# A fused attention, routed experts and gated layer on one core: casts of the last stage's weights on ScalarE, no router places in two blocks, list positions compared in bf16 pairs

## The chip, the cores and the metric

One core of one Trainium2 chip runs the whole program as a single launch. Its engines are TensorE (PE: matmuls, and the weight loads that overlap them), VectorE (DVE), ScalarE (ACT), GpSimd (POOL) and SyncE (SP), each with a queue of instructions of its own that it takes in order, and sixteen DMA engines. The metric is the device time of one execution in microseconds (us), as the median of several.

## The reference

Attention in chunks of 64, a top-1 router with capacities, eight experts, and a layer that takes a maximum over three products:

```python
# q, k, v: [8, 8, 576, 64]
scores = scale * np.matmul(q_c, k_c.transpose(0, 1, 2, 4, 3))   # per chunk of 64
attn = softmax(scores)                                          # written out in the source
out = np.matmul(attn, v_c)
x = attn_out.transpose(0, 2, 1, 3).reshape(4608, 512)

flat = (x @ w_gate).flatten()               # 4608 tokens, 8 experts, cap = 576
for idx in np.argsort(-flat):               # best pairs first
    tok, e = idx // 8, idx % 8
    if assigned[tok] >= 0 or counts[e] >= cap:
        continue
    assigned[tok] = e
    counts[e] += 1
for e in range(8):
    out[mask_e] = np.maximum(x[mask_e] @ w1[e], 0.0) @ w2[e]    # 512 -> 1024 -> 512

h = np.maximum(np.maximum(x @ w1, x @ w2), x @ w3)              # 512 -> 768
return (h @ w_out).astype(np.float32)
```

## The kernel before

All 4608 tokens are first taken through attention (0 to about 169 us). The router then works in rounds: round r fixes which 576 tokens expert r gets, and depends on round r − 1. Round 0 runs alone (169 to about 191 us) on VectorE and PE, while PE is kept busy with filler matmuls ("warm"). The eight experts follow (198 to about 665 us), each with 576 tokens, and the last stage (670 to 1212 us): products of the layer w1, w2, w3 in a scheme with sums of blocks (L1137) and w_out (L1213).

Numbers are split into a high and a low part, and a product is three matmuls: high x high, low weight x high, high weight x low. For the experts, the high part of a weight chunk is a ScalarE cast (L756), the low part a VectorE subtraction (L763). The tokens of an expert are fetched by row with five indirect DMAs on GpSimd (`gather`, L793, with the copies L802 and L803 behind them), transposed on PE (L816, tile pxt, two buffers), cast on ScalarE (xhi, L819) and subtracted on VectorE (xlo, L823). The first layer of an expert (L1044) goes over eight blocks f of 128 hidden units, each in two halves of 288 tokens, 12 matmuls a half; a block's result (acc, two buffers) is evicted by a relu on ScalarE (hhi, L1068) and a subtraction on VectorE (hlo, L1077). In expert 0 the blocks f = 0 and 1 are cut at 256 tokens (`head`), since the last tokens arrive late. The second layer (L1099) goes over four blocks of 48 matmuls, evicted by ScalarE (ys, L1106) and written with a DMA that ScalarE issues (L1107).

Everything else during the experts is put in between by `pump()`, which the loops call after every six matmuls (a "place"). It advances the router (`assigning`: rounds 1 to 7), the gathering and transposing for the next expert (`preparing`), and, as far as a small planner allows, the splits of weight chunks and the conversion of the last stage's weights (`bulk`, `convert`). The planner (`Clock`) counts 800 ns for a place, books VectorE's work at 155 ns an instruction and 1 ns an element, and lets a step of the conversion go when its due time has come and VectorE's booked work fits. So the order of each engine's queue is fixed when the program is written.

A router round, as far as it is touched: the bids (L442 to L446, L516), keys and digits (L486 to L533), five steps, each of comparisons (ge, L537), nine matmuls (L551), cs (L556), four matmuls (L564), fb (L571), a norm's matmul (L580) and lo (L587), and then the lists: positions `at` by a comparison of int32 with a row of 20 numbers (L646), times the column number (L647), times the row number (L649, in round 0 on ScalarE, L651), and 36 matmuls of them (L660).

The conversion takes 6 jobs "o" (blocks of w_out) and 18 jobs "w". A job loads its raw weights by SP, then runs steps ct and cw on ScalarE (L890) and VectorE (L893 to L919), four sums or differences on GpSimd (cw, L926 to L929), and `pair_hi`: high and low parts of seven blocks of 128 columns into the tile pair (one buffer), by GpSimd (L872, L873), and two DMAs to scratch memory (wda, wdb, L876 and L877), also issued by GpSimd. The 18 jobs are numbered in their order, from 1. `pair_hi` of a job is called in the middle of the next one's steps, not before its due time `free[0]`.

## Time and profile before

| | |
|---|---|
| median of 3 runs | 1209.57 us (1208.64 to 1211.05) |
| profiled execution, its own time | 1214.07 us |
| span in the profile | 1212.3 us |
| PE busy | 1175.5 us, 97% of the span |
| VectorE busy | 829.2 us, 68% |
| ScalarE busy | 413.7 us, 34% |
| GpSimd busy | 306.8 us, 25% |
| mean granted PE clock | 0.985 of full speed |

The profiled execution is 4.5 us above the median, and its span leaves out 1.8 us around the first and last instruction. Busy time of PE includes matmuls at a lowered clock. Of the other engines the shares are averages over stages: in the last stage VectorE is about half busy, during the experts 70 to 80% and more in a router round.

### The profile page before, as it was taken

The page shows a single profiled execution, that of the slowest core. Times are in us where ns is not written, and L with a number is a line of the kernel's source. Part 1 is how long each engine was busy: PE and PEld are TensorE (multiplying, and loading weights), DVE is VectorE, ACT ScalarE, POOL GpSimd, SP SyncE. Part 2 cuts the span into 40 slices and gives each one's busy share as a digit, 9 for nine tenths or more (in the row PEclk, how much of TensorE's full clock was granted, in tenths as well). Part 3 has the DMA queues.
Part 4 walks back from the last instruction along what each step waited for, and adds up shares of the span by engine and source line. Part 5 has one row for each costly group of instructions (what it writes and reads, how often), then busy time and mean ns, then how long its engine had stood idle before and what let it go on. Part 6 is the DMA issues. An engine that isn't in the chain of part 4 may idle for free.

```text
span 1212.3 us, 23567 instructions
## 1 busy us (share of the span) xinstructions
PE 1175.5 (97%) x9508; PEld 1098.6 (91%) x9508; DVE 829.2 (68%) x1652; ACT 413.7 (34%) x674; POOL 306.8 (25%) x507
## 2 busy tenths in 40 slices
PE   7899978999999999999999999999999999999998
PEld 6788856999999999998999998998998998998996
DVE  6788976877788888787843565565565565565561
ACT  5788822333333242334432113113113113113111
POOL 7433201010027465745970002002002002002002
PEclk9999978999999999999999999999999999999999
DMA  9999615273556556567654763663763763773651
GB/s 260 246 262 263 175 54 165 89 239 116 187 171 196 190 200 215 172 226 250 222 195 181 270 243 139 269 247 136 270 250 135 270 258 128 274 258 121 230 193 52
DMA packets 138828, 242.99 MB, mean 200 GB/s; under 512 B 30048, under 2 KB 101216, under 8 KB 131808
## 3 DMA queue, kind: packets, MB, share of 16 engines
q1 hardware_dynamic: 118608, 180.90, 45.4%
q0 software_dynamic: 14976, 51.13, 12.5%
q10 hardware_dynamic: 5136, 9.46, 2.1%
q8 instruction: 75, 1.23, 0.4%
q14 instruction: 33, 0.27, 0.1%
HBM read 195.05 MB, written 46.40 MB: 199 GB/s over the span
## 4 chain that ended last, share of the span: by engine, by line
PE 50%; issue 36%; DVE 6%; DMA 4%; POOL 3%; SPq 1%; ACT 1%; POOLq 1%; DVEq 0%; ACTq 0%
PE acc L1099 16%; PE acc L1044 13%; PE pX L181 2%; PE py L1137 2%; POOL out_dram L1221 2%; PE po L1213 2%; PE pT L115 2%; PE px L1137 2%; PE pz L1137 2%; DMA inq<-in_q_dram 2%; PE pS L132 1%; PE pA L168 1%; PE pxt L816 1%; DVE chunk L763 1%; DMA vb<-in_v_dram 1%
## 5 line engine op out<-in xcount | busy, mean ns | idle before, releaser
L1044 PE MATMUL acc<-xhi,chunk 128*128 128x288 f32 (+2 forms) x1024 | 208.1, 302 | 4.8 <-DVE hlo L1077 4.1
L1099 PE MATMUL acc<-hhi,chunk 128*128 128x288 f32 x1024 | 209.9, 299 | 1.3 <-DVE hlo L1077 1.3
L1044 PEld LDWEIGHTS acc<-xhi,chunk 128*128 128x128 f32 x1024 | 161.6, 189 | 6.8 <-DVE hlo L1077 5.0
L1221 POOL DMA_INDIRECT out_dram<-ot,ia x36 | 36.4, 1012 | 516.3 <-ACT ot L1219 515.7
L1099 PEld LDWEIGHTS acc<-hhi,chunk 128*128 128x128 f32 x1024 | 162.9, 188 | 1.9 <-DVE hlo L1077 1.5
L1099 PE MATMUL acc<-hlo,chunk 128*128 128x288 f32 x512 | 150.8, 294 | 0.0
L1213 PE MATMUL po<-chunk,h 128*128 128x512 f32 x648 | 149.3, 390 | 0.0
L1213 PEld LDWEIGHTS po<-chunk,h 128*128 128x128 f32 x648 | 121.5, 188 | 24.8
L1044 PE MATMUL acc<-xlo,chunk 128*128 128x288 f32 (+2 forms) x512 | 143.8, 296 | 0.0
L1137 PE MATMUL px<-xb,wa 128*128 128x384 f32 x648 | 129.9, 334 | 0.7 <-ACT ys L1106 0.7
L1137 PE MATMUL py<-xt,wb 128*128 128x384 f32 x648 | 129.8, 334 | 0.0
L1137 PEld LDWEIGHTS px<-xb,wa 128*128 128x128 f32 x648 | 113.9, 188 | 1.4 <-ACT ys L1106 1.0
L1137 PEld LDWEIGHTS py<-xt,wb 128*128 128x128 f32 x648 | 114.0, 188 | 0.5
L1158 ACT CAST h<-best 128x384 fp32r<-128x384 f32 x72 | 37.0, 514 | 198.1 <-DVE best L1156 121.3
L1099 PEld LDWEIGHTS acc<-hlo,chunk 128*128 128x128 f32 x512 | 96.0, 188 | 0.0
L763 DVE TENSOR_TENSOR chunk<-raw,chunk 128x1024 fp32r<-128x1024 f32 x67 | 86.7, 1299 | 10.8 <-ACT chunk L756 8.0
L1044 PEld LDWEIGHTS acc<-xlo,chunk 128*128 128x128 f32 x512 | 94.1, 189 | 0.0
L1068 ACT ACTIVATE hhi<-acc 128x576 fp32r<-128x576 f32 (+1 forms) x66 | 41.9, 638 | 135.3 <-PE acc L1044 125.0
L793 POOL DMA_INDIRECT xg<-xd,idx x40 | 40.8, 1020 | 152.2 <-DVE ohe L683 75.1
L1173 ACT COPY tmp<-px 128x384 f32<-128x384 f32 x54 | 25.9, 480 | 146.2 <-PE px L1137 146.2
L756 ACT CAST chunk<-raw 128x1024 fp32r<-128x1024 f32 x67 | 69.5, 1047 | 11.3 <-ACT ys L1106 6.0
L1077 DVE SCALAR_TENSOR_TENSOR hlo<-acc,hhi 128x576 fp32r<-128x576 f32 (+1 forms) x66 | 48.3, 735 | 33.0 <-ACT hhi L1068 32.8
(221 smaller groups left out, 2048.1 us busy)
## 6 DMA issues: line engine op xcount, KB each, us to landing
wb<-wdb SPq DMA_DIRECT2D x54, 1024.0 KB
wa<-wda SPq DMA_DIRECT2D x54, 768.0 KB
raw<-in_moe_w_dram SPq DMA_DIRECT2D x64, 512.0 KB
xd<-x POOLq DMA_DIRECT2D x36, 256.0 KB
yd<-ys ACTq DMA_DIRECT2D x32, 288.0 KB
wdb<-pair POOLq DMA_DIRECT2D x18, 512.0 KB
yraw<-yd SPq DMA_DIRECT2D x12, 768.0 KB
ink<-in_k_dram SPq DMA_DIRECT2D x16, 512.0 KB
```

The lines of the kernel that those rows point to most:

```text
L756: nc.scalar.copy(hi, raw)
L763: nc.vector.tensor_tensor(lo, raw, hi.bitcast(F32), op=OP.subtract)
L793: nc.gpsimd.indirect_dma_start(out=g, out_offset=None, in_=xd[:, :], in_offset=bass.IndirectOffsetOnAxis(ap=rt.idx[r][:, t:t + 1], axis=0))
L1044: nc.tensor.matmul(acc[:, hf, :tk.stop - tk.start], w[a][:, dc, o:o + 128], x[:, dc, tk], start=n == 0, stop=n == 11)
L1068: nc.scalar.activation(hv, src, AF.Relu)
L1077: nc.vector.scalar_tensor_tensor(lv, src, 0.0, hv.bitcast(F32), op0=OP.max, op1=OP.subtract)
L1099: nc.tensor.matmul(acc[:, hf, :288], w[a][:, f, :], x[:, f, tk], start=n == 0, stop=n == 23)
L1137: nc.tensor.matmul(dst, w[:, dc, o, a], XO[x][:, c, dc], start=start and n == 0, stop=stop and n == 5, skip_group_check=True)
L1158: nc.scalar.copy(hpart(g, i, j)[0], M)
L1173: nc.scalar.copy(U[g, 1], XB[g])
L1213: nc.tensor.matmul(PO[t], h[:, x, t % 6 * 128:t % 6 * 128 + 128], w[a][:, f % 2], start=f == 0 and n == 0, stop=f == 5 and n == 2)
L1221: st = nc.gpsimd.indirect_dma_start(out=out, out_offset=bass.IndirectOffsetOnAxis(ap=ia[:, t:t + 1], axis=0), in_=ot, in_offset=None)
```

## The change

Three edits. First, in `pair_hi` the high parts are cast by ScalarE in two instructions of 4 and 3 blocks, where GpSimd did it in four; GpSimd keeps the subtractions and the DMAs. Second, `pump` gets an argument, and in expert 0's blocks f = 0 and 1 it doesn't advance the router, which concerns four places. Third, the list positions: the quotient is first cast to bf16 (`qb`), the constants `i20` and `col` are laid out with two columns innermost, and the comparison runs over pairs of columns in bf16; the list matmuls read `tok` accordingly with a stride of two.

```diff
--- before.py
+++ after.py
@@ -365,9 +365,11 @@
         s.i32 = C.tile([128, 32, G], BF, name="i32")
         nc.gpsimd.iota(s.i32, pattern=[[1, 32], [0, G]], base=0, channel_multiplier=0,
                        allow_small_or_imprecise_dtypes=True)
-        s.i20 = io([128, 20], [[1, 20]], name="i20")
-        s.col = C.tile([128, G, 20], BF, name="col")
-        nc.gpsimd.iota(s.col, pattern=[[1, G], [0, 20]], base=0, channel_multiplier=0,
+        s.i20 = C.tile([128, 20, 2], BF, name="i20")
+        nc.gpsimd.iota(s.i20, pattern=[[1, 20], [0, 2]], base=0, channel_multiplier=0,
+                       allow_small_or_imprecise_dtypes=True)
+        s.col = C.tile([128, G // 2, 20, 2], BF, name="col")
+        nc.gpsimd.iota(s.col, pattern=[[2, G // 2], [0, 20], [1, 2]], base=0, channel_multiplier=0,
                        allow_small_or_imprecise_dtypes=True)
         s.row = io([128, 1], [[0, 1]], cm=1, name="row")
         s.w8 = io([128, E], [[-1, E]], base=E, name="w8")
@@ -629,8 +631,10 @@
         nc.vector.tensor_scalar(qi, vi, 5, None, op0=OP.logical_shift_right)
         lists = W.tile([128, 92 * G], BF, name="aoh")
         aoh = lists[:, :32 * G].rearrange("p (j c) -> p j c", c=G)
-        at, tok = lists[:, 32 * G:52 * G], lists[:, 52 * G:].rearrange("p (a c t) -> p a c t", a=2, t=20)
-        at = at.rearrange("p (c t) -> p c t", t=20)
+        at, tok = lists[:, 32 * G:52 * G], lists[:, 52 * G:].rearrange("p (a c t w) -> p a c t w", a=2, t=20, w=2)
+        at = at.rearrange("p (c t w) -> p c t w", t=20, w=2)
+        qb = W.tile([128, G], BF, name="key")
+        nc.vector.tensor_copy(qb, qi)
 
         nc.vector.scalar_tensor_tensor(md, qi, -32.0, vi, op0=OP.mult, op1=OP.add)
 
@@ -643,7 +647,8 @@
             yield 1
         mark("r.tok")
 
-        nc.vector.tensor_tensor(at, bb(qi, 20), s.i20[:, None, :].to_broadcast([128, G, 20]), op=OP.is_equal)
+        nc.vector.tensor_tensor(at, qb.rearrange("p (c w) -> p c w", w=2)[:, :, None, :].to_broadcast([128, G // 2, 20, 2]),
+                                s.i20[:, None].to_broadcast([128, G // 2, 20, 2]), op=OP.is_equal)
         nc.vector.tensor_tensor(tok[:, 0], at, s.col, op=OP.mult)
         if r:
             nc.vector.tensor_scalar(tok[:, 1], at, s.row, None, op0=OP.mult)
@@ -657,7 +662,7 @@
         pi = PS.tile([128, 2, 5, 4], F32, name="rp", tag="rp", bufs=1)
         for c in range(G):
             g = 32 * (c % 4)
-            nc.tensor.matmul(pi[g:g + 32].rearrange("p a t m -> p a (t m)"), aoh[:, :, c], tok[:, :, c],
+            nc.tensor.matmul(pi[g:g + 32].rearrange("p a t m -> p a (t m)"), aoh[:, :, c], tok[:, :, c // 2, :, c % 2],
                              start=c < 4, stop=c >= G - 4, tile_position=(0, g))
         if r > 1:
             yield 1
@@ -867,9 +872,10 @@
         def pair_hi(job):
             mark("conv")
             pair = P.tile([128, 7, 2, 128], F32R, name="pair")
+            for sl in (slice(0, 4), slice(4, 7)):
+                nc.scalar.copy(pair[:, sl, 0], job["cw"][:, sl])
             for o in range(0, 7, 2):
                 sl = slice(o, min(o + 2, 7))
-                nc.gpsimd.tensor_copy(pair[:, sl, 0], job["cw"][:, sl])
                 nc.gpsimd.tensor_tensor(pair[:, sl, 1], job["cw"][:, sl], pair[:, sl, 0].bitcast(F32), op=OP.subtract)
             p, m, dc = job["at"]
             row, flat = (3 * p + m) * 128, pair.rearrange("p o h f -> p (o h f)").bitcast(F32)
@@ -938,12 +944,13 @@
 
     assigning, preparing, converting = assign(), prepare(), convert()
 
-    def pump():
+    def pump(route=True):
 
         state["pump"] += 1
         clock.pe += clock.PLACE
         state["wait"] -= state["wait"] == 1
-        next(assigning, None)
+        if route:
+            next(assigning, None)
         next(preparing, None)
         bulk(clock.PLACE * (min(state["wait"], 2 if state["l1"] else 4) or 2) + 300)
         if state["pump"] % 2:
@@ -1047,7 +1054,7 @@
                         for _ in x_tr(0, xg, [XH[r][2]]):
                             pass
                     if n == 5 and not late:
-                        pump()
+                        pump(not head)
                 if late:
                     if f == 1:
                         for _ in first:
@@ -1070,7 +1077,7 @@
                         state["used"] += 1
                     if f == 7:
                         state["w1"] = r
-                pump()
+                pump(not head)
                 if hf == 1:
                     mark("relu")
                     for src, hv, lv in parts:
```

What it does to the order of instructions, at three places. In the changed kernel the lines have moved by two to seven (L442 is L444 there, L516 L518, L1077 L1084, L580 L582, L551 L553, L816 L821, L1099 L1106, L756 L761, L819 L824, L1106 L1113, L1107 L1114, L872 is L876 on ScalarE, L873 L879).

VectorE in expert 0, where the first two blocks are evicted, with bids of router round 1 (L442 to L516); before:

```order
L689 TENSOR_TENSOR free<-free,outm 128x36
L442 TENSOR_REDUCE bid<-L 128x36
L443 TENSOR_TENSOR t_167<-L,bid 128x288
L444 TENSOR_TENSOR t_167<-t_167,w_113 128x288
L445 TENSOR_REDUCE pr<-t_167 128x36
L446 TENSOR_TENSOR oh<-t_167,pr 128x288
L516 TENSOR_TENSOR bid<-bid,free 128x36
L1077 SCALAR_TENSOR_TENSOR hlo<-acc,hhi 128x256
L1077 SCALAR_TENSOR_TENSOR hlo<-acc,hhi 128x320
```

The same place of VectorE's queue in the changed kernel:

```order
L694 TENSOR_TENSOR free<-free,outm 128x36
L1084 SCALAR_TENSOR_TENSOR hlo<-acc,hhi 128x256
L1084 SCALAR_TENSOR_TENSOR hlo<-acc,hhi 128x320
L1084 SCALAR_TENSOR_TENSOR hlo<-acc,hhi 128x256
L1084 SCALAR_TENSOR_TENSOR hlo<-acc,hhi 128x320
L444 TENSOR_REDUCE bid<-L 128x36
L445 TENSOR_TENSOR t_167<-L,bid 128x288
L446 TENSOR_TENSOR t_167<-t_167,w_113 128x288
L447 TENSOR_REDUCE pr<-t_167 128x36
L448 TENSOR_TENSOR oh<-t_167,pr 128x288
L518 TENSOR_TENSOR bid<-bid,free 128x36
```

The six bid instructions stood ahead of the four subtractions of the two blocks and now stand behind them.

PE at the end of expert 0, where the tokens of expert 1 are transposed (L816) amid the second layer (L1099) and a router step (L580); before:

```order
L580 LDWEIGHTS ones_146
L580 MATMUL rn<-fb,ones_146 128x32
L816 MATMUL pxt<-ident,xg 128x128 x8
L1099 MATMUL acc<-hhi,chunk 128x288 x2
L1099 MATMUL acc<-hlo,chunk 128x288
L1099 MATMUL acc<-hhi,chunk 128x288 x2
```

The same place of PE's queue in the changed kernel, where the second layer is over:

```order
L582 LDWEIGHTS ones_146
L582 MATMUL rn<-fb,ones_146 128x32
L821 MATMUL pxt<-ident,xg 128x128 x8
L553 LDWEIGHTS ge
L553 MATMUL rp<-oh,ge 128x32
```

Before, sixteen rows with 24 matmuls of L1099 stand between these transposes and the nine matmuls of the next step (L551); now the nine (L553) follow at once, and behind them four transposes and six matmuls of expert 1. From there on PE's queue is the same in both kernels.

ScalarE near the end of expert 4, where the tokens of expert 5 are cast (xhi) and a pair is due whose sums GpSimd forms behind the gathers (called job 8 below); before:

```order
L756 CAST chunk<-raw_2957 128x1024
L819 CAST xhi<-pxt 128x4x128 x2
L1106 COPY ys<-acc 128x576
L1107 DMA yd<-ys 128x576
L819 CAST xhi<-pxt 128x4x128 x2
```

The same place of ScalarE's queue in the changed kernel:

```order
L761 CAST chunk<-raw_2957 128x1024
L876 CAST pair<-cw 128x4x128
L876 CAST pair<-cw 128x3x128
L824 CAST xhi<-pxt 128x4x128 x2
L1113 COPY ys<-acc 128x576
L1114 DMA yd<-ys 128x576
```

The pair's two casts are put in ahead of the casts of xhi. Elsewhere in ScalarE's queue, too, the 36 casts are the only difference. In GpSimd's queue the casts are gone; a job's subtractions stand where they stood among the other GpSimd instructions.

## Rows read from the trace of the kernel before

**Rows 1.** PE's waits, 190 to 670 us: tile, releaser, us in total, times, longest
```profile
PE acc L1044 <- DVE hlo L1077: 4.1, 3, 2.4
PE rp L564 <- DVE cs L556: 1.9, 2, 1.6
PE pxt L816 <- DVE xlo L823: 1.4, 3, 0.6
PE acc L1099 <- DVE hlo L1077: 1.3, 1, 1.3
...
PE rn L580 <- DVE fb L571: 0.6, 2, 0.3
```

**Rows 2.** groups by line (busy us, mean ns | idle before, releaser): the list positions
```profile
L646 DVE TENSOR_TENSOR aoh<-vq,i 128x720 bf16<-128x720 int32 x8 | 7.5, 934 | 0.0
...
L647 DVE TENSOR_TENSOR aoh<-aoh,col 128x720 bf16<-128x720 bf16 x8 | 4.3, 533 | 0.3
...
L533 DVE CAST key<-ki 128x36 bf16<-128x36 int32 x7 | 1.2, 174 | 0.0
```

**Rows 3.** timeline of expert 0: start, us, engine, instruction, [idle before <- releaser]
```profile
207.41 1.54 DVE L1077 SCALAR_TENSOR_TENSOR hlo<-acc,hhi 128x256 fp32r<-128x256 f32 x4
...
208.28 0.54 PE L1044 MATMUL acc<-xhi,chunk 128*128 128x288 f32 x2 [1.30 <-DVE hlo L1077]
```

**Rows 4.** timeline of PE and VectorE, boundary from expert 0 to expert 1
```profile
256.87 0.19 PE L580 MATMUL rn<-fb,ones 128*128 128x32 bf16 x1
...
257.58 0.83 DVE L537 TENSOR_TENSOR ge<-key,lev 128x640 bf16<-128x640 bf16 x2
...
258.32 1.28 DVE L823 TENSOR_TENSOR xlo<-pxt,xhi 128x512 fp32r<-128x512 f32 x2
```

**Rows 5.** groups by line: a weight block's work on GpSimd and ScalarE, and the relu
```profile
L873 POOL TENSOR_TENSOR pair<-cw,pair 128x256 fp32r<-128x256 f32 x72 | 56.2, 781 | 5.8
...
L1068 ACT ACTIVATE hhi<-acc 128x576 fp32r<-128x576 f32 (+1 forms) x66 | 41.9, 638 | 135.3 <-PE acc L1044 125.0 <-PE rn L580 10.2
...
L872 POOL CAST pair<-cw 128x256 fp32r<-128x256 f32 x72 | 40.0, 556 | 18.8 <-DMA wdb<-pair 18.6
...
L890 ACT ACTIVATE ct<-c 128x512 f32<-128x512 f32 x24 | 16.2, 673 | 2.1 <-DVE cw L919 1.7 <-ACT ys L1106 0.5
```

**Rows 6.** timeline of GpSimd and VectorE, expert 4, job 7
```profile
456.21 0.74 POOL L873 TENSOR_TENSOR pair<-cw,pair 128x256 fp32r<-128x256 f32 x1
...
456.27 1.76 DVE L763 TENSOR_TENSOR chunk<-raw,chunk 128x1024 fp32r<-128x1024 f32 x1
...
456.89 1.40 POOL L872 CAST pair<-cw 128x256 fp32r<-128x256 f32 x1
...
463.94 1.21 DVE L763 TENSOR_TENSOR chunk<-raw,chunk 128x1024 fp32r<-128x1024 f32 x1
```

**Rows 7.** timeline of PE, two of its idle times
```profile
512.31 0.24 PE L564 MATMUL rp<-cs,lev 128*128 128x8 f16 x4 [1.59 <-DVE cs L556]
...
570.93 0.53 PE L1044 MATMUL acc<-xhi,chunk 128*128 128x288 f32 x2 [2.40 <-DVE hlo L1077]
```

**Rows 8.** windows: length, busy us (count) of PE, PEld, DVE, ACT, POOL, clock, DMA, GB/s
```profile
510.00:514.00 4.00, 2.41 (x22) 2.27 (x20) 3.97 (x7) 0.44 (x1) 3.84 (x6) 1.00 0.01 4
572.00:576.00 4.00, 4.00 (x20) 4.00 (x20) 3.82 (x5) 0.07 (x1) 2.86 (x6) 0.57 0.69 257
```

**Rows 9.** timeline of GpSimd, ScalarE and PE around job 8
```profile
481.00 0.59 POOL L803 COPY ia<-idx 64x4 int32<-64x4 int32 x1 [5.25 <-DMA xg<-xd,idx]
...
482.49 1.08 ACT L819 CAST xhi<-pxt 128x512 fp32r<-128x512 f32 x2 [2.12 <-PE pxt L816]
...
483.51 0.53 POOL L929 TENSOR_TENSOR cw<-cw 128x128 f32<-128x128 f32 x1
...
486.17 1.07 PE L816 MATMUL pxt<-ident,xg 128*128 128x128 f32 x8
```

**Rows 10.** which engine waited for whom, whole span: a pair's buffer
```profile
POOL pair L872 <- DMA wdb<-pair: 18.6, 9, 5.4
```

## The prediction

> **What bounds the kernel now.** TensorE (PE) is busy for 97% of the span, so an edit on another engine counts only where PE waits for that engine. I read two views, in this order. First PE's waits during the experts, 190 to 670 us, the only stage that the change touches besides the first router round: nearly all of them end with VectorE (DVE), and the four largest groups of them sum to 4.1 + 1.9 + 1.4 + 1.3 = 8.7 us [rows 1]. Everything that the change can give back in this stage is therefore about 9 us, plus what a long idle costs in clock. Second, the timeline around each of those waits, for what made VectorE late. What the reader should see there: VectorE is seldom idle and seldom short of an input; it is held up by work of lower urgency ahead in its queue (the router's), or by an instruction that takes longer while GpSimd (POOL) runs.
>
> The last stage (670 to 1212 us) has the same instructions in the same order before and after, so I give it nothing.
>
> **Part 3, the list positions.** The comparison L646 reads int32 and takes 0.934 us; the multiplication L647, as wide and all bf16, takes 0.533 us. The new cast of 36 numbers is like L533, 0.174 us [rows 2]. If the compare in bf16 pairs runs as the multiplication does, a round saves 0.934 − 0.533 − 0.174 = 0.23 us; if it stays at 0.93 us, the cast is added, +0.2. Only round 0 lies on the path (PE has only filler there); rounds 1 to 7 lie beside matmuls of the experts. The other operand of the list matmuls is now read with a stride; no row shows that, and I bound it by doubling 36 short matmuls of 40 columns, at most +0.5, and take 0. **Term: −0.2 us** (−0.2 to +0.7).
>
> **Part 2, no router places in expert 0's first blocks.** PE idles 1.30 us at 208.28 because the residual subtraction L1077 (hlo) begins at 207.41 only [rows 3]: it stands behind six bid instructions of router round 1 that the four places have brought forward. In the new order four of L1077 stand ahead of them, so this idle goes: −1.3. Short ones of up to 0.3 us in the blocks behind it, each for a router step (two of them are the fifth row of [rows 1]), would fall elsewhere; I count −0.4. But the round now begins 24 matmuls later, and is back in step at the boundary to expert 1. There PE had 24 matmuls between the norm's matmul L580 and the next nine L551; now it has eight transposes (L816), then L551. After L580 at 256.87 the comparison L537 runs from 257.58 for 0.83, so it is done 258.41, or 1.54 us after L580; PE is through with its transposes about 0.9 us after it (eight take 1.07 with their start-up [rows 9]). That is 0.6 us of idle. Then four transposes wait for two residual subtractions (L823), which run 1.28 us in a row from 258.32 [rows 4]: some 0.45 us more, and 0.25 for the step L564 behind them, +1.3 together. **Term: −1.3 − 0.4 + 1.3 = −0.4 us** (−1.7, were the boundary hidden, to +0.9, if the whole chain of the round comes through with its three steps).
>
> **Part 1, the casts.** GpSimd loses 72 casts, 40.0 us, and keeps 72 subtractions, 56.2 us. ScalarE gains 18 casts of 512 elements, like L890 at 0.673 us, and 18 of 384, three quarters of that: 18 x (0.673 + 0.505) = 21 us [rows 5] on an engine with a third of the span busy. Where ScalarE isn't on time the price isn't these 21 us but a wait; two steps below.
>
> What VectorE gains: at 456.27 a chunk split L763, 1.21 us where nothing is in its way (463.94), took 1.76 us while a subtraction of GpSimd's (456.21, 0.74 us) ran, and GpSimd's cast at 456.89 took 1.40 instead of 0.40 us beside the split [rows 6]. So the two hold each other up whichever is first. With the casts gone a job is 3 instead of 5 us of this on GpSimd, and since the subtraction waits for ScalarE's cast, several jobs move, by the place of ScalarE's casts in the new order: job 7 by about ten microseconds, out of the stretch of [rows 6], jobs 10 and 11 by about three. For the waits this means, one by one: all of the 1.3 us of the fourth row of [rows 1], 1.3 of the 1.59 us at 512.31, 0.7 of the 2.40 us at 570.93 [rows 7] (VectorE is behind there, 3.82 of the 4 us after it busy [rows 8], and the part of the job that stays is the larger), the 0.4 us that is the third of that group [rows 1], and all of the 1.4 us of L816. Sum 1.3 + 1.3 + 0.7 + 0.4 + 1.4 = **−5.1 us** (between 0 and −7.1, which is the 8.7 without the 1.3 us of part 2 and 0.3 us of its short ones). After the 2.40 us idle the granted clock is 0.57 for 4 us, little over the lower of its two levels (1.2 of 2.4 GHz); in 510 to 514, around the 1.59 us idle, it stays at 1.00 [rows 8]. Four microseconds at 0.57 instead of 1 cost 1.7. An idle of 1.7 us is next to the second row, but nothing lies between; I take half, **−0.9 us** (0 to −1.7).
>
> The Trainium skill speaks against this term: its page "SBUF — State Buffer", section "Who interferes with whom", says that a VectorE instruction with two SBUF inputs and a GpSimd one that reads SBUF take turns, the later one blocked until the first is done. The rows above agree (1.76 for 1.21 us). By that rule the subtractions that remain block as before, and what goes is the casts' share only; this is the first rival below.
>
> What ScalarE makes late: at job 8 its casts stand ahead of the four xhi casts that the next transposes wait for. They need the sums cw of GpSimd (L926 to L929), and these stand behind the copy L803, which waits 5.25 us, till 481.00, for the gathers to land; the last sum starts at 483.51 [rows 9]. Job 7's four subtractions, now just ahead of these gathers, take away what earlier work would win them, so I leave 481.00 where it is, while PE by then is 1.9 us earlier (0.2 + 0.4 + 1.3). The first cast starts at about 483.5, the second ends 484.7 (it needs the last sum, done 484.04), two xhi at 0.54 end 485.2 and 485.8, and the residual of the first frees PE's transposes at 485.9. Before, they started at 486.17, now they are due 486.17 − 1.9 = 484.3 [rows 9]: **+1.65 us** (0.3 if the gathers also come earlier; 3.5 with the clock lost, 1.65 + 1.7, and no more since two buffers take the rest). For the other 17 jobs I followed ScalarE's order: 14 stand where it is idle, and three wait up to about 2 us for the write of the previous pair to finish, less or hardly more than ScalarE's mean idle of 125.0 / 66 = 1.9 us ahead of a relu L1068 [rows 5]. Taken as 0.
>
> **Sum.** −0.2 − 0.4 − 5.1 − 0.9 + 1.65 = −4.95 us. The profiled execution took 1214.07 us (a span of 1212.3), so by its own time 1209.1. It was 4.5 us above the median of the runs shown, 1209.57; I apply the difference to the median: **1204.6 us.** By the best ends (−0.2 − 0.4 − 7.1 − 1.7 + 0.3) it is 1200.5.
>
> **Rivals.** *VectorE's delays only move* (the same, 1209.8 us). The subtractions stay, 56.2 of 96.2 us [rows 5], and are what held up the split at 456.27 [rows 6]; moved by some microseconds they meet other splits. Then half of 5.1 is won, the idle at 570.93 stays long enough to lose its clock, and job 8 costs its idle and the clock: −0.2 − 0.4 − 2.55 + 1.65 + 1.7 = +0.2. For it: a chunk split is in each stretch. Against it: PE waits only where a router step and a job meet, and these places were few.
>
> *ScalarE waits for the pair's write* (slower, 1213.9 us). The pair has one buffer. GpSimd waited nine times, 18.6 us in all, 5.4 at the longest, for the write to scratch to leave it, [rows 10], and nobody stood behind it. Now ScalarE takes this wait, in order, with relu, chunk casts and evictions behind it. Half of it on the path is +9.3 on the forecast; it decides for slower once 40% of 18.6 us (7.4) ends on PE. Against it: ScalarE's idle ahead of each relu is 1.9 us, and the new order puts most casts later than GpSimd's were.
>
> *The compare in pairs isn't faster:* +0.4 on the forecast, 1205.0, no other sign.
>
> **How the numbers follow.** A measurement of this kernel tells about 0.2% from no change, 2.4 us. Forecast 0.60 (its own ends 1200.5 to 1207.1), the delays that move 0.27, ScalarE's wait 0.13. So faster 0.60, same 0.27, slower 0.13. The range reaches from the sum's best end over the first rival: 1200.5 to 1210.5, leaving out most of the slower case and the little below.
>
> **What would show it.** Right: the compare near 0.53 us; PE's wait at 208 gone and one of 0.6 us at about 257; the waits of 1.3, 1.59 and 0.4 to 0.6 us gone or under 0.3; a new wait of some 1.65 us for an xlo or xhi near 484; the clock kept near 570. Wrong: the sum of PE's waits for VectorE at 6 us or more (first rival), or waits of PE for hhi, xhi or chunks that end with a ScalarE cast which waited for the pair's write (second).

## The result, and where the time went

The changed kernel takes 1219.45 us (1218.67 to 1221.81, 6 runs) against 1210.73 for the kernel before (1208.64 to 1212.52, 6 runs): a ratio of 1.0074, with an interval of 1.0060 to 1.0088. It is slower by 8.7 us, where 5 us less was forecast.

The changed kernel's page, part 1, busy us by engine, its share of the span of 1217.6 us and the count of instructions:

```profile
PE 1176.5 (97%) x9508; PEld 1099.8 (90%) x9508; DVE 826.0 (68%) x1660; ACT 429.5 (35%) x710; POOL 273.2 (22%) x435
```

Work moved as written: GpSimd 33.6 us less, ScalarE 15.8 us more, VectorE 3 us less, TensorE the same. None of this says why it is slower; the waits do. PE's waits from 185 to 680 us in the changed kernel (tile, releaser, us in total, times, longest), to be read against [rows 1]:

```profile
PE pxt L821 <- DVE xlo L828: 5.0, 4, 3.2
PE acc L1051 <- DVE hlo L1084: 4.7, 3, 1.9
PE rp L566 <- DVE cs L558: 2.3, 4, 0.8
PE rp L553 <- DVE ge L539: 1.5, 3, 0.7
PE acc L1051 <- DVE chunk L768: 1.3, 1, 1.3
```

The 1.3 us of L1099 is gone, as are the 1.59 us of L564 and the 2.40 us of hlo as single waits. In their place the wait for xlo went from 1.4 to 5.0 us, hlo is waited for no less than before (4.7 for 4.1), and ge and a chunk, which hardly held PE up before, appear.

The attention part isn't touched by any edit, yet it ends between 163 and 170 us in the profiled executions of this study. So I compare stages: round 0 of the router from its first product to the first matmul of expert 0, then each expert from its first matmul of layer 1 to the next one's. All are start times from the timeline of PE; us:

| kernel | round 0 | e0 | e1, e2 | e3 | e4 | e5 | e6 | e7 | sum |
|---|---|---|---|---|---|---|---|---|---|
| before | 28.73 | 63.35 | 115.84 | 57.56 | 59.36 | 61.02 | 58.93 | 51.76 | 496.55 |
| changed | 28.36 | 65.45 | 115.83 | 58.18 | 63.92 | 61.39 | 60.36 | 51.77 | 505.26 |
| difference | −0.37 | +2.10 | 0.0 | +0.62 | +4.56 | +0.37 | +1.43 | 0.0 | +8.71 |

The last stage takes 546.2 us before and 546.1 after. The sum of the differences, 8.71 us, agrees with the measured one (8.72) by luck to the hundredth: each row is one execution with its own clock, and in other kernels below the sum is off from the medians by up to 4.3 us (part 1 alone: 4.19 against 8.45). But it tells where to look: expert 0 (part 2), expert 4 (job 8) and expert 6 have most of it.

**Expert 4.** Timeline of GpSimd, ScalarE and PE of the changed kernel around job 8, the lines that answer to [rows 9]:

```profile
475.24 1.91 POOL L798 DMA_INDIRECT xg<-xd,idx  x1 [0.30 <-issue]
...
483.24 0.18 POOL L808 COPY ia<-idx 64x4 int32<-64x4 int32 x1 [5.71 <-DMA xg<-xd,idx]
...
484.94 1.04 ACT L876 CAST pair<-cw 128x512 fp32r<-128x512 f32 x2 [6.88 <-POOL cw L934]
...
485.88 1.06 ACT L824 CAST xhi<-pxt 128x512 fp32r<-128x512 f32 x2
...
487.24 1.97 PE L821 MATMUL pxt<-ident,xg 128*128 128x128 f32 x8 [3.24 <-DVE xlo L828]
```

ScalarE stands 6.88 us before a cast whose input GpSimd forms only once the gathers have landed; xhi, xlo and the transposes follow one behind the other, and PE idles 3.24 us. Expert 4 starts at 434.05 us here and at 435.05 before, so times are compared from its start. The gathers landed 3.24 us later than before (49.19 against 45.95 us): their first issue starts 0.77 later, the five issues take 1.9 longer in all (0.94 to 1.91 us each, before 0.94 to 1.16), and the landing 0.6. The four kernels of this study with job 7's casts on ScalarE and pairs 14 places apart have these five lengths to within 0.02 us, the others don't; why the issues take longer there, no run shows. The clock fell with this idle. One window of the changed kernel behind it (length, busy us and count of PE, PEld, DVE, ACT, POOL, then granted clock, DMA share, GB/s):

```profile
487.00:493.00 6.00, 5.76 (x29) 5.61 (x30) 4.32 (x8) 2.61 (x4) 2.26 (x5) 0.53 0.73 225
```

Expert 4 without the old wait of 1.28 us and with 3.24 us would be 59.36 − 1.28 + 3.24 = 61.32; it took 63.92. The 2.6 us more fit those six microseconds at 0.53 of the clock (an estimate: 6 x 0.47 = 2.8).

**Expert 6.** Timeline of the changed kernel, ScalarE, VectorE, PE:

```profile
579.50 1.03 ACT L876 CAST pair<-cw 128x512 fp32r<-128x512 f32 x2 [5.41 <-DMA wdb<-pair]
...
580.44 0.64 ACT L1075 ACTIVATE hhi<-acc 128x576 fp32r<-128x576 f32 x1
...
581.12 0.76 DVE L1084 SCALAR_TENSOR_TENSOR hlo<-acc,hhi 128x576 fp32r<-128x576 f32 x1 [3.04 <-ACT hhi L1075]
581.93 0.53 PE L1051 MATMUL acc<-xhi,chunk 128*128 128x288 f32 x2 [1.84 <-DVE hlo L1084]
```

This is the second rival's chain: a cast waits for the write of the previous pair, the relu behind it is late, VectorE waits for the relu, PE for VectorE. It ends one of three waits of PE's in expert 6. The others, 0.99 us ahead of it and 1.91 us behind it (before 2.40 and 0.41), end with a VectorE that worked without a break from 570.39 and from 582.05 us on, until the subtraction that PE waits for. The second stretch begins with splits of chunks that ScalarE cast behind the pair, so the 1.91 may come of the same chain. What waits for a pair in the whole changed kernel, in answer to [rows 10]:

```profile
POOL pair L879 <- ACT pair L876: 82.2, 15, 9.6
...
ACT pair L876 <- DMA wdb<-pair: 16.1, 4, 5.4
...
ACT pair L876 <- POOL cw L934: 6.9, 1, 6.9
```

GpSimd's 18.6 us have become ScalarE's 16.1 us, now with PE's evictions behind them.

**Expert 0.** Timeline of VectorE and PE of the changed kernel, at the first chunk and at the end of expert 0, in answer to [rows 3, 4]:

```profile
209.92 1.22 DVE L768 TENSOR_TENSOR chunk<-raw,chunk 128x1024 fp32r<-128x1024 f32 x1
...
211.19 0.40 PE L1051 MATMUL acc<-xhi,chunk 128*128 128x288 f32 x1 [1.27 <-DVE chunk L768]
...
255.05 0.24 PE L566 MATMUL rp<-cs,lev 128*128 128x8 f16 x4 [0.77 <-DVE cs L558]
...
258.69 0.60 PE L553 MATMUL rp<-oh,ge 128*128 128x32 bf16 x9 [0.75 <-DVE ge L539]
...
259.63 0.66 PE L821 MATMUL pxt<-ident,xg 128*128 128x128 f32 x4 [0.33 <-DVE xlo L828]
```

The idle of 1.30 us, before at 9.98 us from the start of expert 0, is gone. At 16.60 us PE stands 1.27 us for a chunk that VectorE splits behind the same bids, digits and comparisons (before, 0.25 us for this chunk). A wait of 0.49 us for cs comes at 33.81 us, and at the end of expert 0 the three waits shown.

### The profile page after: what moved, and what is told of

Same layout as the page of the kernel before. It is cut to its first block, busy times and chain, and to the rows that moved or that the text cites. A ratio compares the mean times of both kernels' runs of the same rounds, so it can differ in the third digit from the quotient of the medians.

```text
span 1217.6 us, 23561 instructions
## 1 busy us (share of the span) xinstructions
PE 1176.5 (97%) x9508; PEld 1099.8 (90%) x9508; DVE 826.0 (68%) x1660; ACT 429.5 (35%) x710; POOL 273.2 (22%) x435
## 4 chain that ended last, share of the span: by engine, by line
PE 48%; issue 36%; DVE 5%; POOL 3%; DMA 3%; ACT 2%; SPq 2%; another core or an unknown queue 1%; POOLq 1%; ACTq 0%; DVEq 0%
PE acc L1051 14%; PE acc L1106 13%; PE pX L181 3%; PE py L1144 2%; POOL out_dram L1228 2%; PE pT L115 2%; PE po L1220 2%; PE pS L132 2%; PE pA L168 2%; PE px L1144 2%; PE pz L1144 2%; PE pxt L821 1%; DMA raw<-in_moe_w_dram 1%; PE pY L199 1%; DVE chunk L768 1%
## 5 line engine op out<-in xcount | busy, mean ns | idle before, releaser
L1106 PE MATMUL acc<-hhi,chunk 128*128 128x288 f32 x1024 | 211.5, 301 | 0.0
L1106 PEld LDWEIGHTS acc<-hhi,chunk 128*128 128x128 f32 x1024 | 164.2, 189 | 0.4
L1106 PE MATMUL acc<-hlo,chunk 128*128 128x288 f32 x512 | 151.3, 296 | 0.0
L1106 PEld LDWEIGHTS acc<-hlo,chunk 128*128 128x128 f32 x512 | 96.7, 189 | 0.0
L768 DVE TENSOR_TENSOR chunk<-raw,chunk 128x1024 fp32r<-128x1024 f32 x67 | 84.2, 1261 | 17.3 <-ACT chunk L761 14.2
L879 POOL TENSOR_TENSOR pair<-cw,pair 128x256 fp32r<-128x256 f32 x72 | 58.9, 848 | 82.4 <-ACT pair L876 82.2
L761 ACT CAST chunk<-raw 128x1024 fp32r<-128x1024 f32 x67 | 69.5, 1047 | 10.3 <-ACT ys L1113 6.0
```

The lines of the kernel that those rows point to most:

```text
L761: nc.scalar.copy(hi, raw)
L768: nc.vector.tensor_tensor(lo, raw, hi.bitcast(F32), op=OP.subtract)
L879: nc.gpsimd.tensor_tensor(pair[:, sl, 1], job["cw"][:, sl], pair[:, sl, 0].bitcast(F32), op=OP.subtract)
L1106: nc.tensor.matmul(acc[:, hf, :288], w[a][:, f, :], x[:, f, tk], start=n == 0, stop=n == 23)
```

## The experiments

Line numbers differ by a few from kernel to kernel; the text names what the lines do.

### The parts, each alone

Part 1 alone: the kernel before with the casts on ScalarE, no other edit.

```diff
+            for sl in (slice(0, 4), slice(4, 7)):
+                nc.scalar.copy(pair[:, sl, 0], job["cw"][:, sl])
...
-                nc.gpsimd.tensor_copy(pair[:, sl, 0], job["cw"][:, sl])
```

> The kernel before with part 1 alone (casts on ScalarE). By the stages of the two traces part 1 has cost: expert 3 +0.6, expert 4 +4.6, expert 5 +0.4, expert 6 +1.4 us. Theory A (the parts add up; the cost is ScalarE standing in order behind a cast that waits): +6 to +7.5 us on the kernel before, ratio 1.005 to 1.006, with PE's idle of about 3.2 us for xlo near 487 us and waits for hlo in expert 6. Rival B (the parts interact: the waits of part 1 arise only because part 2 shifted router round 1): within 2 us of the kernel before.

1219.71 us (4 runs) against 1211.26 (for each run, the kernel before on the same chip), ratio 1.0084 (1.0062 to 1.0106); an idle of 3.17 us for xlo at 488, and 2.13 and 1.92 us for hlo in expert 6. Rival B, that part 2 brought these waits about, falls: part 1 has them by itself. In this execution the same idle left the clock alone (the window behind it):

```profile
488.00:494.00 6.00, 5.97 (x49) 5.65 (x50) 5.21 (x11) 3.20 (x6) 3.81 (x8) 1.00 0.77 230
```

and expert 4 took 61.66 us, not 63.92. Its profiled execution (1217.56 us) is the fastest of its four.

Part 2 alone, four places without the router:

```diff
-                        pump()
+                        pump(not head)
...
-                pump()
+                pump(not head)
```

> The kernel before with part 2 alone (no router places in the first two blocks). Theory A: +2 us (expert 0 took 63.35 us before and 65.45 after: the 1.30 us idle is gone, a wait of 1.27 us for a chunk and 1.85 us at the end of expert 0 have come), ratio 1.0017. Rival B: the end of expert 0 was late because of ScalarE's or GpSimd's moved work; then the 1.3 us is won and the time is 1 to 1.5 us below the kernel before.

1211.72 against 1211.26, ratio 1.0007 (0.9989 to 1.0025): in the times not to be told from no change. The trace tells more: expert 0 took 65.45 us, to the hundredth what it takes in the changed kernel, with the same waits (1.28 for the chunk, 0.49, and 0.75, 0.74, 0.33 at the end). So the 2.1 us come with part 2 without the others, and rival B falls. The sum of stages is 496.72 us, only 0.2 more than before, since expert 6 took 57.33 instead of 58.93: its idle of 2.19 us (2.40 before) left the clock at 1.00, for part 2 or by chance; the runs don't tell.

Part 3 alone: the diff's edits to `i20`, `col`, `qb`, `at` and the list matmuls.

> The kernel before with part 3 alone (positions in bf16 pairs). Theory A: -0.4 us from the first router round alone, not to be told from no change in the times; the comparison at about 0.53 us in the trace, and PE's waits in experts 1 to 7 as before within 0.5 us. Rival B (a faster comparison moves VectorE's work against the matmuls enough to matter): over 1.5 us either way.

1207.83 against 1211.26, ratio 0.9984 (0.9970 to 0.9998). That is rival B's size (over 1.5 us), not theory A's: experts 4 to 6 gained 0.28, 0.45 and 1.87 us. Round 0 is shorter by 0.36 us, as expected, but it takes 28.41 to 28.73 us in the five kernels without part 3 and 28.30 to 28.63 in seven of the eight with it (29.73 in the eighth, at a lower clock), so this isn't shown. PE's waits from 190 to 670 us in this kernel:

```profile
PE acc L1050 <- DVE hlo L1083: 4.1, 3, 1.9
PE rp L566 <- DVE cs L558: 1.6, 2, 1.0
PE acc L1105 <- DVE hlo L1083: 1.0, 1, 1.0
PE pxt L821 <- DVE xlo L828: 0.8, 2, 0.5
```

VectorE has little slack there, and a round's work on the lists is shorter by 0.14 us (0.560 + 0.533 + 0.236 against 0.934 + 0.533). The wait of 1.28 became 0.97 and that of 1.59 became 1.05, and so they are in the run with part 3 and the half of part 2; one of 0.29 became 0.55. In expert 6 nothing can be put down to part 3: 2.40 became 1.89, but the two kernels with part 2 alone or by half have 2.19 and 1.80, and like part 3 alone they kept the clock at 1.00 and take 57.33 and 56.92 us there, where part 3 alone takes 57.06. So of the 3.0 us in the stages some 0.7, in experts 4 and 5, can be put down to part 3; the medians say 3.4, with an interval of about 0.2 to 3.6.

### Load of ScalarE, or its place in the queue

The changed kernel, with job 8's casts on GpSimd again:

```diff
+            late8 = job["at"] == (1, 0, 1)
-            for sl in (slice(0, 4), slice(4, 7)):
+            for sl in () if late8 else (slice(0, 4), slice(4, 7)):
...
+                if late8:
+                    nc.gpsimd.tensor_copy(pair[:, sl, 0], job["cw"][:, sl])
```

> The changed kernel, but the casts of job 8 alone are GpSimd's again, so that ScalarE doesn't stand behind the gathers there. Theory A (order): PE's idle of 3.24 us near 487 and the low clock behind it go, 5 to 6 us less than the changed kernel, about 1213.9. Rival C (load: 21 us more on ScalarE make it late everywhere): only an eighteenth of the loss goes, under 0.5 us, and the idle near 487 stays over 2 us.

1212.88 us (10 runs), 6.6 us less than the changed kernel; against the kernel before 1.0024 (1.0005 to 1.0043), where the changed kernel has 1.0074. One job of eighteen made two thirds to three quarters of the loss. ScalarE's xhi cast is on time again:

```profile
480.27 1.07 ACT L824 CAST xhi<-pxt 128x512 fp32r<-128x512 f32 x2 [2.13 <-PE pxt L821]
```

and expert 4 takes 58.04 us, 1.3 us less than before: the old wait of 1.28 us near 464, which job 7's move did take away. In the stages of this execution expert 6 is 2.5 us shorter too (no wait of PE's there cost the clock) and round 0 1.4 longer (a lower clock). The load theory falls: the other 17 jobs' casts are still on ScalarE.

The changed kernel, with pairs further apart:

```diff
-            free[0] = clock.pe + 14 * clock.PLACE
+            free[0] = clock.pe + 20 * clock.PLACE
```

> The changed kernel with the next pair due 20 places after the last one's, in place of 14, so that a pair's write has landed and the gathers are through when ScalarE comes to its casts. Theory A (ScalarE's waits in order are the cost): no wait of ScalarE's casts over 1 us ahead of a relu or xhi cast, the idle of 3.24 us near 487 and those of 1.84 and 1.91 us in expert 6 gone; experts 4 to 6 no longer than before, 7 to 9 us below the changed kernel, about 1211. Rival C (load of ScalarE, or GpSimd's moved subtractions beside VectorE): experts 4 to 6 stay over 3 us longer than in the kernel before.

1213.98 us, 5.5 less than the changed kernel where 7 to 9 were expected; ratio to before 1.0022 (1.0006 to 1.0038). Partly as theory A has it: experts 4 to 6 take 58.88, 59.75 and 55.00 us, 173.6 together, where the kernel before takes 179.3 and the changed one 185.7. But the last pairs crowded into the end of expert 7's first layer, and expert 7 takes 58.70 instead of 51.76. Timeline of ScalarE and PE there:

```profile
647.01 1.03 ACT L876 CAST pair<-cw 128x512 fp32r<-128x512 f32 x2 [13.05 <-DMA wdb<-pair]
...
648.63 0.85 PE L1106 MATMUL acc<-hhi,chunk 128*128 128x288 f32 x2 [4.77 <-ACT ys L1113]
```

The same wait, in another place: ScalarE 13.05 us for a pair's write, then an eviction (ys) behind it, PE 4.77 us.

Two limits of this run. A pair's due time also holds back the last steps of the next job on VectorE and its sums on GpSimd, so 20 places move more than ScalarE's casts; the kernel before with 20 places wasn't run. And expert 0 takes 64.37 us here, 1.1 less than in the changed kernel, though the first pair comes in expert 2 only and the programs are the same up to there. Timeline of ScalarE near the end of expert 0, the changed kernel first, this run second:

```profile
250.42 0.64 ACT L1113 COPY ys<-acc 128x576 f32<-128x576 f32 x1 [7.39 <-remote]
...
247.37 0.64 ACT L1113 COPY ys<-acc 128x576 f32<-128x576 f32 x1 [5.38 <-PE acc L1106]
```

From the start of expert 0 (194.59 and 193.50 us) these are 55.83 and 53.87 us. PE's block ends at 53.8 us in both; in the changed kernel the eviction starts 2.0 us later, for a release that the profile puts down to no instruction ("remote"), and behind it stand chunk casts, chunk splits and the cs that PE waits for. Part 2 alone has it too (55.83). In this run the waits of 0.77 and 0.75 us are gone and one of 0.74 for xlo is left. So expert 0 with part 2 can take 64.4 or 65.5 us from the same instructions.

### How much part 1 could win at VectorE

The kernel before without any of GpSimd's pair work. It leaves out casts and subtractions of the last stage's weights, of which zeros are written.

```diff
-            pair = P.tile([128, 7, 2, 128], F32R, name="pair")
-            for o in range(0, 7, 2):
-                sl = slice(o, min(o + 2, 7))
-                nc.gpsimd.tensor_copy(pair[:, sl, 0], job["cw"][:, sl])
-                nc.gpsimd.tensor_tensor(pair[:, sl, 1], ...)
...
+        pair = P.tile([128, 7, 2, 128], F32R, name="pair")      # once
+        nc.gpsimd.memset(pair.bitcast(F32), 0.0)
```

> The kernel before without GpSimd's 144 casts and subtractions for the pairs (the pair is zeroed once; the last stage's weights and the output are thus left out). The ceiling of what part 1 could have won at VectorE. Theory A (GpSimd's work stretches VectorE and makes PE wait): of the 8.7 us of PE's waits for VectorE in experts 4 to 6 at least 5 go, and the clock stays at the idle of 2.40 us: 5 to 8 us below the kernel before. Rival D (VectorE is late in a router round by its own queue): 5 us or more of these waits stay, less than 3 us below.

1203.99 against 1211.27, ratio 0.9954 (0.9939 to 0.9970): 7.3 us in the times, 8.3 in the stages (488.21 against 496.55). PE's waits from 190 to 670 us, all that involve VectorE:

```profile
PE acc L1041 <- DVE hlo L1074: 2.6, 2, 1.3
...
PE rn L580 <- DVE fb L571: 0.6, 2, 0.3
...
PE acc L1041 <- DVE chunk L763: 0.3, 1, 0.3
PE rp L564 <- DVE cs L556: 0.2, 1, 0.2
PE pxt L816 <- DVE xlo L823: 0.2, 1, 0.2
```

Theory A holds: of the waits in experts 4 to 6 (7.4 us before, as 1.30 of the 8.7 lie in expert 0) one of 1.31 us is left, and nothing else over 0.25. They were GpSimd's doing. But this takes away the subtractions too, and part 1 leaves them. What they do by themselves the changed kernel shows in expert 3, where 0.62 us were lost and no cast waited; timeline of GpSimd, VectorE, PE:

```profile
415.54 2.56 POOL L879 TENSOR_TENSOR pair<-cw,pair 128x256 fp32r<-128x256 f32 x4
415.56 2.15 DVE L493 TENSOR_SCALAR ki<-ki 128x36 int32<-128x36 int32 x3
...
417.83 0.97 DVE L539 TENSOR_TENSOR ge<-key,lev 128x640 bf16<-128x640 bf16 x2
...
418.52 0.60 PE L553 MATMUL rp<-oh,ge 128*128 128x32 bf16 x9 [0.19 <-DVE ge L539]
```

and the same digits where GpSimd is idle, in expert 0 of the same kernel:

```profile
208.61 0.45 DVE L493 TENSOR_SCALAR ki<-ki 128x36 int32<-128x36 int32 x4
```

Three tiny instructions take 2.15 us beside four subtractions in a row; four of them take 0.45 us otherwise. The Trainium skill ("SBUF — State Buffer", section "Who interferes with whom") states that a VectorE instruction in a two-port mode, which tensor_scalar can enter, and a GpSimd instruction block each other, the first to come for its whole length. The rows agree in kind (2.15 us for three, 0.45 us for four); that these three ran in such a mode no run shows. Without the casts between them GpSimd's subtractions follow each other directly.

### Part 2 by half

```diff
                     if n == 5 and not late:
-                        pump()
+                        pump(not head)
```

Only the two places in the middle of the blocks skip the router.

> Part 2 alone and by half: only the two places in the middle of the two blocks skip the router, those at a block's end don't. Theory A (what stands ahead of the first blocks' subtraction is only moved ahead of the chunk's split, and the round comes late by as many places): the idle of 1.30 us at 208 is shorter or gone, the wait for a chunk is shorter than 1.27 us, and the end of expert 0 costs about 1 us less than with four places; expert 0 between 63.3 and 64.8 us (63.35 before, 65.45 with part 2). Rival E (any shift of round 1 against the transposes of expert 1 costs the same): 65 us or more.

1211.53 against 1211.27, ratio 1.0006 (0.9986 to 1.0025). The times show no gain, the stage does: expert 0 takes 62.59 us, 0.76 less than before and 2.86 less than with four places. The idle at 208 stayed (1.28 us), against what theory A had; gone are the short ones of 0.25 and 0.28 us, and the end of expert 0 costs nothing, since the round is only two places late and still has matmuls of the second layer between its steps. What part 2 gains in expert 0 is lost by its last two places. The stages of this execution sum to 493.36 us, 3.2 less than before, 2.0 of it in expert 6; the medians have none of that, so a difference of 2 us in expert 6 of one execution says little of an edit.

### Toward a better version

Part 3, and of part 1 the casts of job 7 alone:

```diff
+            act = job["at"] == (1, 0, 0)
+            for sl in (slice(0, 4), slice(4, 7)) if act else ():
+                nc.scalar.copy(pair[:, sl, 0], job["cw"][:, sl])
...
+                if not act:
+                    nc.gpsimd.tensor_copy(pair[:, sl, 0], job["cw"][:, sl])
```

> Part 3, and of part 1 the casts of job 7 alone on ScalarE, the one job whose move took a wait of PE's away (1.28 us near 464 in the kernel before). Theory A: that wait goes, nothing else moves: 1 to 1.3 us below part 3 alone, 3 to 4.5 us below the kernel before, ratio 0.9965 to 0.9975. Rival D: job 7's subtractions, now beside the gathers of the next expert, push those back and PE waits for the tokens near 486: no gain against part 3 alone.

1209.39 against 1211.27, ratio 0.9981 (0.9965 to 0.9998). Expert 4 gains 1.26 us on part 3 alone (57.82 against 59.08), as expected, but expert 5 takes 61.40 instead of 60.57. Two thirds come back as waits one expert later: here the first rival's sentence, that the delays only move, is what happens. The ratio is outside the expected 0.9965 to 0.9975 and that of part 3 alone (0.9984): in the times nothing is gained on it. Rival D's gathers do come late (they land at 49.31 us of expert 4, with part 3 alone at 46.81), but PE doesn't wait for them.

Part 3 and the half of part 2, without part 1 (the two edits shown above):

> Part 3 and the half of part 2 (two places in the middle of the blocks), without part 1. Theory A (stages add up): expert 0 at 62.6, the other stages as with part 3 alone; router round 0 and the experts together 492.8 us (496.55 in the kernel before, 493.57 with part 3 alone), 2 to 4 us below the kernel before. If the two meet in expert 1 or later: over 494.

1208.29 against 1210.77, ratio 0.9982 (0.9967 to 0.9998); stages 492.87 us where 492.8 was expected. In the stages the two add up; in the times (part 3 alone had 0.9984) the 0.7 us between them can't be seen.

Parts 1 and 3, the half of part 2, and two distances between pairs:

```diff
-            free[0] = clock.pe + 14 * clock.PLACE
+            free[0] = clock.pe + (20 if (3 * p + m) * 2 + dc < 10 else 14) * clock.PLACE
```

> Parts 1 and 3 and the half of part 2, with 20 places from a pair to the next for the first ten jobs and 14 for the rest. Theory A (what part 1 wins at VectorE was there, and was eaten by ScalarE's waits): experts 4 and 5 as in the run with 20 places throughout, 58.9 and 59.8 us (59.36 and 61.02 before), expert 7 at 51.8 again since the last pair isn't crowded into its end, expert 6 between 55 and 57; in all 489 to 491.5 us against 496.55, time about 1204 to 1206. Rival F (the last pairs at 14 places bring ScalarE's waits back in expert 6): expert 6 at 58 or more.

1214.15 against 1210.77, ratio 1.0024 (1.0012 to 1.0035). Experts 4 and 5 are at 58.91 and 59.77 us and expert 7 at 51.77, as forecast; expert 6 takes 62.66, so rival F holds. Timeline of ScalarE and PE:

```profile
575.99 1.03 ACT L876 CAST pair<-cw 128x512 fp32r<-128x512 f32 x2 [6.91 <-DMA wdb<-pair]
...
581.94 0.85 PE L1051 MATMUL acc<-xhi,chunk 128*128 128x288 f32 x2 [7.20 <-DVE hlo L1084]
```

One wait of ScalarE's, 6.91 us, ahead of a chunk's cast and a relu, and PE stands 7.20 us.

The same with 12 in place of 10 in the edit:

> As the run before it, with 20 places for the first twelve jobs; the last cast now stands at the end of expert 7's first layer. Theory A: expert 6 nearer 55 us, expert 7 between 51.8 and 53.5; in all 489 to 492 us. Rival G (a cast at the end of expert 7's first layer already costs what it did with 20 places throughout, 6.9 us): expert 7 over 56 us.

1205.11 us (5 runs) against 1210.77, ratio 0.9962 (0.9939 to 0.9984): faster than both kernels. Expert 6 takes 55.10 us and expert 7 52.12; the stages sum to 490.98, where 489 to 492 was expected. ScalarE's waits for a pair's write, the last of the 18 at the end of the first layer of expert 7 included:

```profile
ACT pair L876 <- DMA wdb<-pair: 6.2, 4, 2.6
```

That is 1.9 us less than the version without part 1 (492.87), and 3.2 us less in the medians. How much of it the casts on ScalarE make, and how much the 20 places, isn't shown: the version with 20 places and the casts on GpSimd wasn't run.

## Why the prediction was wrong

Four steps failed: that ScalarE's waits for a pair's write cost nothing (measured: waits of up to 5.41 us, and PE behind them); that the gathers at job 8 land when they did (3.24 us later); that relief at VectorE is counted wait by wait where GpSimd's work leaves; and that an eviction put ahead of the router's work wins PE's idle.

**What bounds it, and where.** Right: PE's waits for VectorE in experts 4 to 6 came from GpSimd, and were worth some 9 us with the clock; without the pair work 7.3 us went in the times and 8.3 in the stages. The last stage and experts 1 and 2 did not move.

**Part 3** (−0.2 us): the right sign, too small, and by another way. In the changed kernel the rows that answer to [rows 2] are

```profile
L650 DVE TENSOR_TENSOR aoh<-key,i 128x720 bf16<-128x720 bf16 x8 | 4.8, 595 | 0.0
L652 DVE TENSOR_TENSOR aoh<-aoh,col 128x720 bf16<-128x720 bf16 x8 | 4.7, 586 | 0.3
L637 DVE CAST key<-vq 128x36 bf16<-128x36 int32 x8 | 1.5, 183 | 0.3
```

(columns: busy us, mean ns | idle before). The comparison runs at the multiplication's rate. With the cast the three take 1.36 us a round against 1.47, so 0.10 us is saved where 0.23 was worked out (0.14 in part 3 alone). The step that failed is "rounds 1 to 7 lie beside matmuls": in rounds whose stretch has a wait of PE's for VectorE they lie on the path, and experts 4 and 5 gave 0.7 us with part 3 alone; in round 0, where the term was looked for, no gain stands out.

**Part 2** (−0.4 us, measured +2.1): the idle of 1.30 went, as said, and the end of expert 0 cost 0.77 + 0.75 + 0.33 = 1.85 us where 1.3 was worked out, the wait for cs ahead of L580 being left out. Of these 1.85 us some 1.1 hang on the eviction that started 2.0 us late, since the run with 20 places, the same up to there, has 0.74 instead and takes 64.37 us: without that lateness part 2 costs 1.0 us. The short waits, −0.4 in the sum, gave nothing: 0.28 went and 0.49 came, and the second of the two in [rows 1] lies at the end of expert 1, where it stayed (0.27 in both kernels). The step that failed is the first: an idle that VectorE's queue causes isn't won by putting the eviction ahead of the router's work, as long as the next thing that PE needs of VectorE, the chunk, stands behind the same work. 1.02 of the 1.30 us (1.27 − 0.25) came back 6.6 us on.

**Part 1, relief** (−5.1 and −0.9 us): 1.28 us went in expert 4. In expert 3 0.62 were lost and in expert 5 0.37. In expert 6 the clock fell as before (0.57 for 4 us), behind another idle. The term took each wait of [rows 1] and asked whether its GpSimd job moved; it did not ask what stands where the job moves to. In the best version, with ScalarE's waits short, the casts' move and the new distance between pairs together brought 1.9 us, less than half of the term. This is the first rival's mechanism, to which 0.27 was given; it took half off the term, and that was too little.

**Part 1, job 8** (+1.65 us, up to 3.5 with the clock; 485.9 − 484.3 is 1.6 and 1.65 + 1.7 is 3.35): the chain was right link by link, its size wasn't. I left the gathers' landing where it was, on the ground that job 7's subtractions only cancel a gain; counted from the start of expert 4 it came 3.24 us later. The links behind the landing took 4.00 us (483.24 to 487.24), where 4.9 were worked out. So the idle became 3.24. With the clock expert 4 lost 3.24 + 2.6 = 5.8 us in the profiled execution, over the upper end; job 8 alone is 6.6 us in the medians (1219.45 against 1212.88).

**Part 1, the other jobs** (0): wrong in expert 6. I compared ScalarE's mean idle ahead of a relu (1.9 us) with waits of "up to about 2 us", although [rows 10] said 5.4 for the longest, and the changed kernel has 5.41. A mean slack covers no longest wait. Of the three waits in expert 6 this chain ends the one of 1.84 us and may be behind that of 1.91; with 20 places, where more than the casts moves, the expert takes 55.0 us instead of 60.36. The second rival named this mechanism; 0.13 was too little for it, as job 8 is of the same kind (ScalarE in order behind a cast that waits) and had been found already.

So the measured sum is −0.4 (round 0) + 2.1 + 0.6 + 4.6 + 0.4 + 1.4 = +8.7 us. The forecast's −4.95 fails by 2.5 in part 2 (2.10 − (−0.4)), and by nearly all of the rest in part 1. The range ended at 1210.5, because ScalarE's waits had been put into a rival as a whole instead of onto the sum's upper end, one by one.

What stays open: why expert 6's idle of 2.40 us cost the clock in the profiled execution of the kernel before (1.7 us by the row in [rows 8]), and similar ones did not in other kernels; and therefore how much of any gain in that expert is an edit's own. Open too: what held the eviction at the end of expert 0 for 2.0 us, why the gathers' issues took longer, and what the casts' move is worth by itself with pairs 20 places apart.

## What to carry to other kernels

Moving work to an engine with two thirds of its time free is not priced by its busy time but by the longest wait of the moved instruction, since everything behind it in that queue waits too; so put a moved instruction where its input and its buffer are ready (here, in the fastest version, 20 places between the first pairs instead of 14), or leave it on the engine that nobody waits for. Where PE idles for a late VectorE, look at the next two things that PE takes from it before counting the idle as won. When one job in eighteen is found to stand badly, look at the longest wait, not at the mean, for the others.

## What the runs showed of the hardware

- An idle of PE costs its clock in one execution and not in another: 3.24 us of idle in the changed kernel were followed by 0.53 for six microseconds, 3.17 us with part 1 alone by 1.00; 2.40 us in the kernel before cost it, 2.19 us with part 2 alone didn't, 1.91 us in expert 6 of the changed kernel, five microseconds behind another of 1.84, did:

```profile
588.00:592.00 4.00, 4.00 (x21) 4.00 (x20) 3.72 (x5) 1.03 (x2) 1.46 (x2) 0.57 0.30 120
```

  The two levels are 1.2 and 2.4 GHz, so 0.53 and 0.57 are little over the lower one. In these cases the length of the idle alone doesn't decide.
- GpSimd's subtractions take from VectorE's smallest instructions, not only from its large ones: three instructions on 36 columns took 2.15 us beside four subtractions, four of them 0.45 us without.
- The issue of a gather on GpSimd took 0.94 to 1.91 us in the same group of five (0.94 to 1.16 in the kernel before), the same lengths in four kernels; the five took 1.9 us longer, and the landing, counted from the start of expert 4, came 3.24 us later.
- One eviction on ScalarE started 2.0 us after the recorded end of the matmuls that it waits for, in three kernels at the same place, and at their end in a fourth with the same instructions up to there.
